# Keys in three tiles of 128 and a shared tile of 64, in place of four tiles of 112, in an attention-then-MLP kernel

## The chip, the cores and the metric

The kernel runs on one core of one Trainium2 chip. The metric is device microseconds of one execution, taken as the median of three runs. Smaller is better. The kernel reads its inputs from HBM in float32, works on them in bfloat16 on TensorE (PE) with float32 sums, and writes float32.

## What is computed

There are 8 batches of 12 heads; each head has 448 rows of 64 numbers. Queries and keys are normalised, attention follows, and the heads of a token, side by side (768 numbers), go through an MLP with a hard-swish.

```python
def rmsnorm(x, g):
    return x / np.sqrt(np.mean(x * x, axis=-1, keepdims=True) + 1e-06) * g
q_n, k_n = rmsnorm(q, g_q), rmsnorm(k, g_k)        # q, k, v: (8, 12, 448, 64)
scores = np.matmul(q_n, k_n.transpose(0, 1, 3, 2)) / np.sqrt(64)
attn = softmax(scores)                              # over the 448 keys
x = np.matmul(attn, v).transpose(0, 2, 1, 3).reshape(3584, 768)
h = x @ w_in                                        # w_in: (768, 2048)
out = (h * np.clip(h + 3.0, 0.0, 6.0) / 6.0) @ w_out  # w_out: (2048, 768)
```

## The kernel before

**Work by pairs and batches.** Two heads form a pair; there are 6 pairs to a batch and 48 in all, numbered `P`. Once the six pairs of a batch are through attention, its 448 token rows are complete and its part of the MLP can run. Attention of later batches and MLP of earlier ones are woven together on PE.

**One pair, step by step.** `load` brings queries, keys and values of the pair into SBUF, one transfer of 256 KB for each, on SP's queue. Partition `p` holds rows `4p` to `4p+3` of each head, so a head's 448 rows lie on 112 partitions by 4. `prep` squares (`sq`, L401 on ACT, L403 on POOL), sums (`ssq`, L410 on DVE), takes the power -1/2 by a logarithm and an exponential on ACT (`rs`, L415 and L418) and scales into bfloat16 (`qks`, L427, mostly POOL). It also casts the values into `va`, which has a 65th column of ones, so that the sum of the softmax falls out of the same product. `trans` turns queries and keys so that the 64 numbers of a head lie on partitions: for `P` under 13 with PE (L479) and a copy out of PSUM, later with a transposing DMA from SP (L455) and a scaling in place (L464 or L466). Head 0 lies on partitions 0 to 63 of `T`, head 1 on 64 to 127.

`score` takes one key tile (112 keys, loaded as 128 columns) of both heads: two matmuls of 64 rows, one on each half of the PE array, with 448 query columns each (L510). ACT takes the exponential of both at once, 112 partitions by 896 columns (`eT`, L519). `av` multiplies one key tile's exponentials by the values: for each of 2 heads and 4 query tiles one matmul of 65 columns that sums into `X` (L531). `finish` takes the reciprocal of the 65th column (`rd`, L547), scales (`xn`, L550) and transposes into `xT`, with PE and a copy for the first two batches (L566) and with a transposing DMA later (L557).

**The MLP.** `h_group` makes one of 16 blocks of 128 hidden columns for a batch: 6 matmuls of 448 columns (L587), a RELU on ACT (`ts`, L594), a product on DVE (`gT`, L597). `y_group` makes 128 output rows of two batches: two halves of 384 columns, 16 matmuls each (L618), a copy and a store (L639). `w_in` and `w_out` arrive in four chunks each. POOL issues them, in line with its arithmetic (L653, L658); the chunk of `w_out` with hidden blocks `4c` to `4c+3` is needed by the `c`-th four matmuls of every half.

**PSUM.** Two score tiles `S` of two banks each, the two-bank `X`, and two single banks `M` for the MLP. From pair 24 on, one score tile in four is put into `X` while that is free, so that up to three score tiles stand next to each other.

**Order.** Nothing is decided at run time. `Plan.add` records every operation with the engines that may do it and their planned costs; `WAY` says which of these engines takes it, and `ORDER` is the full list of operations as they are emitted. Each engine executes its own in that order, and a dependency keeps it so.

Of the kernel before, what the change touches and what calls it, by code (L numbers as in the profile page):

```python
# [21 lines left out]
WAY = {53: 1, 63: 2, 67: 1, 68: 1, 69: 1, 78: 1, 83: 1, 84: 1, 95: 1, 101: 1, 126: 1, 132: 2, 157: 1,  # L22
    163: 1, 183: 1, 188: 1, 225: 1, 231: 1, 233: 1, 245: 1, 250: 1, 256: 1, 276: 1, 358: 1, 365: 1, 377: 1,
    388: 1, 400: 1, 424: 2, 429: 1, 446: 1, 453: 1, 458: 1, 460: 1, 487: 1, 500: 1, 505: 1, 516: 1, 518: 1,
    533: 1, 625: 1, 636: 1, 676: 1, 683: 2, 709: 2, 714: 1, 728: 1, 729: 1, 755: 1, 761: 2, 766: 1, 793: 1,
    798: 1, 821: 1, 892: 1, 899: 2, 925: 2, 930: 1, 945: 1, 951: 2, 977: 2, 1003: 2, 1008: 1, 1023: 1,
    1029: 1, 1034: 1, 1061: 1, 1097: 1, 1134: 1, 1148: 1, 1182: 2, 1206: 1, 1212: 1, 1226: 1, 1251: 1,
    1257: 2, 1263: 1, 1398: 1, 1413: 1, 1420: 2, 1426: 1, 1440: 1, 1447: 1, 1453: 1, 1464: 1, 1465: 1,
    1491: 1, 1515: 1, 1516: 1, 1522: 1, 1549: 1, 1555: 1, 1579: 1, 1615: 1, 1620: 1, 1652: 1, 1673: 1,
    1693: 1, 1700: 1, 1706: 1, 1718: 1, 1724: 2, 1744: 1, 1751: 2, 1757: 1, 1781: 1, 1795: 1, 1832: 1,  # L30
    1893: 1, 1921: 1, 1932: 1, 1938: 1, 1958: 1, 1971: 1, 1979: 1, 1980: 1, 1986: 1, 1992: 1, 2057: 1,
    2062: 1, 2093: 1, 2098: 1, 2125: 1, 2145: 1, 2162: 1, 2169: 1}


class Plan:

# [8 lines left out]
    def add(self, ways, want, fn, reads=(), writes=(), load=(), since=0.0, soon=()):  # L49
        i = len(self.ops)  # L50
        self.way[i] = WAY.get(i, 0)
        eng, occ, fin = ways[self.way[i]]
        soon = dict(soon)
        preds = {}

        def after(p, lat):
            preds[p] = max(preds.get(p, 0.0), lat)

        for r in reads:
            if r in self.last:  # L60
                after(*self.last[r])
            self.readers.setdefault(r, []).append((i, fin))
        for w in writes:
            for p in self.readers.get(w, ()):
                if p[0] != i:
                    after(*p)
            if w in self.last:
                after(*self.last[w])
        for w in writes:
            self.last[w] = (i, soon.get(w, fin))  # L70
            self.readers[w] = []
        self.ops.append((eng, occ, fin, want, fn, preds, load, since))
        self.ways.append(ways)
        return i

    def emit(self, order):

        place = {i: n for n, i in enumerate(order)}
        assert len(place) == len(self.ops)
        for i, o in enumerate(self.ops):  # L80
            assert all(place[p] < place[i] for p in o[5])
        for i in order:
            self.ops[i][4](self.ops[i][0])
# [3 lines left out]
    8, 9, 20, 13, 21, 22, 15, 23, 11, 24, 28, 10, 25, 19, 29, 53, 26, 12, 30, 27, 14, 54, 31, 16, 55, 32, 33,  # L87
    34, 17, 58, 35, 56, 36, 83, 37, 92, 38, 78, 59, 39, 60, 40, 57, 62, 41, 18, 69, 42, 43, 44, 61, 45, 93,
    68, 66, 46, 73, 47, 67, 64, 123, 48, 101, 70, 49, 50, 74, 122, 65, 75, 71, 63, 77, 104, 72, 217, 102, 84,
    105, 76, 81, 85, 154, 51, 103, 112, 94, 124, 82, 79, 52, 86, 114, 80, 113, 153, 126, 115, 110, 87, 95,  # L90
    155, 135, 88, 111, 96, 91, 89, 136, 106, 116, 184, 117, 107, 133, 97, 118, 90, 143, 119, 185, 156, 108,
    134, 132, 120, 186, 144, 109, 141, 121, 248, 142, 145, 146, 166, 98, 1, 157, 164, 147, 167, 158, 148, 99,
    165, 174, 163, 149, 215, 137, 150, 159, 172, 100, 125, 387, 138, 151, 175, 127, 0, 139, 216, 173, 218,
    140, 187, 152, 195, 128, 197, 188, 129, 196, 176, 177, 178, 198, 130, 179, 189, 203, 160, 204, 205, 131,
    246, 180, 168, 181, 190, 206, 161, 169, 170, 247, 182, 171, 191, 183, 162, 228, 385, 226, 229, 207, 194,
    208, 386, 201, 227, 199, 192, 209, 416, 202, 210, 200, 236, 211, 234, 225, 212, 237, 230, 414, 219, 213,
    249, 259, 214, 231, 6, 220, 238, 260, 239, 193, 235, 445, 267, 2, 221, 232, 240, 222, 268, 241, 257, 223,
    242, 233, 243, 415, 258, 250, 261, 244, 262, 245, 265, 256, 251, 277, 266, 278, 224, 269, 279, 280, 281,
    443, 252, 396, 388, 253, 397, 263, 270, 271, 264, 255, 272, 398, 285, 286, 273, 287, 274, 288, 254, 289,
    401, 275, 444, 389, 402, 395, 399, 276, 390, 400, 3, 290, 282, 406, 291, 407, 5, 391, 403, 292, 392, 283,  # L100
    472, 405, 394, 297, 284, 298, 404, 393, 293, 299, 408, 294, 417, 502, 300, 425, 295, 418, 305, 426, 296,
    306, 4, 427, 419, 501, 301, 307, 302, 420, 430, 308, 428, 421, 303, 409, 422, 431, 313, 429, 424, 473,
    446, 314, 423, 304, 432, 410, 315, 411, 309, 433, 316, 310, 474, 434, 412, 321, 413, 311, 322, 312, 454,
    323, 531, 447, 435, 455, 436, 324, 317, 456, 448, 318, 329, 319, 503, 475, 459, 449, 457, 320, 450, 437,
    460, 438, 330, 452, 458, 439, 440, 453, 325, 331, 451, 461, 530, 332, 462, 441, 326, 476, 442, 463, 337,
    338, 477, 327, 7, 483, 339, 464, 328, 484, 621, 465, 504, 466, 340, 467, 478, 333, 485, 468, 482, 469,
    486, 345, 479, 487, 480, 488, 346, 489, 470, 622, 534, 490, 347, 471, 491, 334, 348, 481, 493, 492, 494,
    495, 335, 496, 512, 336, 647, 533, 497, 513, 341, 498, 342, 535, 514, 499, 515, 343, 517, 516, 344, 648,
    536, 505, 354, 537, 518, 506, 539, 349, 500, 350, 538, 507, 351, 508, 649, 509, 519, 520, 522, 523, 510,
    355, 521, 356, 511, 524, 541, 544, 625, 525, 542, 526, 527, 543, 357, 699, 540, 352, 358, 635, 624, 528,  # L110
    546, 353, 529, 547, 674, 366, 650, 626, 361, 548, 360, 651, 367, 627, 673, 676, 368, 652, 628, 532, 677,
    549, 632, 700, 633, 550, 630, 678, 551, 552, 369, 634, 629, 553, 362, 679, 554, 675, 370, 637, 653, 545,
    654, 661, 728, 363, 655, 638, 555, 378, 556, 656, 639, 379, 701, 636, 380, 687, 703, 680, 658, 752, 659,
    364, 681, 623, 640, 660, 726, 641, 365, 631, 642, 381, 702, 371, 729, 663, 382, 730, 751, 373, 664, 682,
    374, 665, 704, 375, 731, 889, 732, 684, 662, 705, 727, 685, 561, 643, 686, 562, 644, 645, 376, 706, 372,
    563, 734, 688, 689, 713, 377, 690, 666, 893, 667, 564, 668, 669, 725, 691, 557, 708, 683, 558, 646, 755,
    670, 671, 710, 657, 559, 890, 569, 733, 711, 560, 570, 672, 892, 707, 565, 712, 894, 891, 566, 571, 692,
    739, 693, 567, 694, 572, 695, 895, 915, 715, 896, 568, 716, 577, 696, 709, 578, 753, 717, 573, 383, 714,
    754, 574, 579, 736, 384, 697, 575, 737, 580, 718, 698, 719, 756, 720, 738, 585, 765, 586, 576, 757, 918,
    359, 721, 758, 741, 587, 722, 723, 742, 735, 581, 588, 759, 582, 724, 743, 740, 744, 593, 583, 941, 760,  # L120
    762, 584, 967, 763, 594, 944, 589, 903, 764, 897, 590, 968, 595, 745, 767, 591, 898, 916, 596, 768, 746,
    592, 747, 601, 919, 748, 769, 749, 602, 993, 766, 761, 597, 603, 920, 900, 750, 901, 770, 771, 772, 604,
    969, 773, 902, 598, 774, 775, 994, 970, 609, 921, 599, 899, 610, 922, 776, 924, 600, 905, 611, 908, 906,
    909, 612, 923, 605, 917, 904, 907, 606, 955, 617, 607, 618, 1019, 608, 945, 926, 619, 946, 942, 613, 927,
    910, 943, 911, 928, 620, 614, 996, 912, 929, 781, 947, 913, 948, 615, 997, 931, 925, 1020, 932, 934, 616,
    935, 950, 914, 782, 998, 933, 936, 949, 1021, 777, 783, 937, 999, 784, 778, 1000, 938, 952, 939, 779,
    1146, 1001, 789, 953, 956, 940, 790, 1002, 780, 954, 791, 951, 981, 1148, 971, 785, 1147, 786, 972, 957,
    787, 960, 958, 961, 1197, 788, 792, 1022, 930, 1196, 794, 793, 973, 1149, 959, 795, 1145, 796, 1023, 1150,
# [79 lines left out]
def kernel(  # L208
# [84 lines left out]
    for t in T_r:  # L293
        nc.vector.memset(t[:, S2:], 0.0)
    for t in eT_r:
        nc.vector.memset(t[:, :, S2:], 0.0)
# [485 lines left out]
```

## Time and profile before

| | |
|---|---|
| time of three runs | 429.72, 429.72, 430.66 us; median 429.72 us |
| span of the profiled execution, first to last instruction | 427.8 us |
| PE busy | 415.1 us (97%), granted clock 1.000 |
| ACT, DVE, POOL busy | 296.7, 219.6, 171.1 us |
| chain that ended last | PE 90%, ACT 4%, issue 2% |
| DMA | 67.77 MB, 158 GB/s over the span |

The profile records one execution, whose span is 427.8 us; no time of its own is listed beside that. The median of the three runs is 1.9 us above the span, and this is taken for what lies around the span (start and end of the program). PE's busy time is modelled from starts, since matmuls are pipelined: a matmul of 448 columns shows 353 ns by itself, while six of them in a row take 1.14 us in the chain, 190 ns each. Costs of PE are therefore read from the chain, not from the mean of a group.

### The profile page before, as it was taken

The numbers are of one execution on the slowest core, as the hardware profiler recorded it, in microseconds if no ns is written. First come the engines' busy times: TensorE is split into PE (matmuls) and PEld (weight loads), VectorE is DVE, ScalarE is ACT, GpSimd is POOL, SyncE is SP. The second block draws the span as 40 slices with busy tenths as digits, with TensorE's granted clock in tenths as the row PEclk, the third lists the DMA queues.
The fourth block names the chain that finished last, engine by engine and source line by source line (L and its number), as shares of the span: only waits on it lengthen the run. The fifth ranks groups of instructions, "written<-read, shape, count | busy, mean of one in ns | idle before, by whom it ended". The sixth has DMA issues, their size and how long they took to land.

```text
span 427.8 us, 9914 instructions
## 1 busy us (share of the span) xinstructions
PE 415.1 (97%) x3946; PEld 238.6 (56%) x3946; DVE 219.6 (51%) x405; ACT 296.7 (69%) x535; POOL 171.1 (40%) x188
## 2 busy tenths in 40 slices
PE   9678999999999999999999999999999999999996
PEld 8455455555555555555555555555555555655554
DVE  5665776547787965665545454434434332243211
ACT  5999898889998988968757977575575556222221
POOL 2899865874767866255524340312200000000000
PEclk9999999999999999999999999999999999999999
DMA  8999999698799999668565865352413221021113
GB/s 258 349 249 288 242 240 250 149 267 231 197 237 262 229 234 227 187 155 233 136 170 132 215 156 124 75 125 55 93 33 70 50 60 49 11 75 37 38 38 113
DMA packets 98931, 67.77 MB, mean 158 GB/s; under 512 B 53156, under 2 KB 95428, under 8 KB 98884
## 3 DMA queue, kind: packets, MB, share of 16 engines
q1 hardware_dynamic: 93248, 60.50, 54.5%
q0 software_dynamic: 5248, 6.29, 8.4%
q8 instruction: 31, 0.51, 0.5%
q10 hardware_dynamic: 388, 0.34, 0.3%
q14 instruction: 16, 0.13, 0.1%
HBM read 50.23 MB, written 11.01 MB: 143 GB/s over the span
## 4 chain that ended last, share of the span: by engine, by line
PE 90%; ACT 4%; issue 2%; DVE 1%; DMA 1%; POOL 1%; SPq 0%; POOLq 0%
PE M L587 32%; PE M L618 29%; PE X L531 10%; PE S L510 8%; PE S L618 5%; ACT eT L519 2%; PE X L587 1%; DMA qk<-in_k_dram 1%; PE S L587 1%; PE X L510 1%; PE X L618 1%; POOL qks L427 1%; DVE gT L597 0%; SPq L388 0%; ACT ts L594 0%
## 5 line engine op out<-in xcount | busy, mean ns | idle before, releaser
L519 ACT ACTIVATE eT<-S 112x896 bf16<-112x896 f32 x168 | 148.1, 918 | 13.8 <-PE S L510 13.3
L587 PE MATMUL M<-xT,w_in_sb 128*128 128x448 bf16 x714 | 153.2, 353 | 0.8 <-ACT xT L347 0.4
L618 PE MATMUL M<-w_out_sb,gT 128*128 128x384 bf16 x752 | 135.9, 326 | 0.0
L597 DVE SCALAR_TENSOR_TENSOR gT<-ts,M 128x448 bf16<-128x448 f32 x119 | 73.4, 619 | 101.9 <-ACT ts L594 101.7
L427 POOL TENSOR_TENSOR qks<-qk,rs 112x512 bf16<-112x512 f32 x94 | 96.2, 1043 | 65.5 <-DMA T<-qks 31.9
L618 PEld LDWEIGHTS <-gT 128*128 128x128 bf16 x912 | 84.8, 98 | 61.9 <-issue 9.7
L594 ACT ACTIVATE ts<-M 128x448 f32<-128x448 f32 x119 | 64.8, 548 | 61.0 <-PE M L587 59.8
L587 PEld LDWEIGHTS <-w_in_sb 128*128 128x128 bf16 x768 | 69.9, 98 | 65.7 <-issue 10.9
L403 POOL TENSOR_TENSOR sq<-qk 112x512 f32<-112x512 f32 x56 | 57.7, 1041 | 43.4 <-DMA qk<-in_k_dram 18.2
L531 PEld LDWEIGHTS <-eT 112*128 112x128 bf16 x1536 | 57.1, 97 | 18.1 <-issue 8.2
L410 DVE TENSOR_REDUCE ssq<-sq 112x16 f32<-112x1024 f32 (+1 forms) x50 | 57.9, 1172 | 15.8 <-ACT sq L401 11.9
L531 PE MATMUL X<-va,eT 112*128 112x65 bf16 x1536 | 62.3, 194 | 1.0 <-DVE xT L349 0.8
L510 PE MATMUL S<-T 64*128 64x448 bf16 x336 | 47.3, 354 | 2.1 <-ACT eT L519 1.5
L550 DVE TENSOR_TENSOR xn<-X,rd 112x512 bf16<-112x512 f32 x48 | 33.2, 691 | 1.6
L351 POOL CAST va<-vf 112x512 bf16<-112x512 f32 x20 | 12.3, 613 | 41.1 <-PE X L531 38.8
L510 PEld LDWEIGHTS <-T 64*128 64x128 bf16 x384 | 12.8, 94 | 27.9 <-issue 21.0
L401 ACT ACTIVATE sq<-qk 112x512 f32<-112x512 f32 x40 | 24.9, 629 | 4.7 <-DMA qk<-in_q_dram 2.3
L347 ACT COPY y<-M 128x384 f32<-128x384 f32 x26 | 12.5, 481 | 18.4 <-PE M L618 18.1
L547 DVE RECIPROCAL rd<-X 112x8 f32<-112x8 f32 x48 | 9.8, 204 | 28.1 <-PE X L531 27.9
L349 DVE COPY y<-M 128x384 f32<-128x384 f32 x21 | 11.7, 555 | 22.8 <-PE M L618 22.6
L519 ACT ACTIVATE eT<-X 112x896 bf16<-112x896 f32 x24 | 22.1, 923 | 0.0
L618 PE MATMUL S<-w_out_sb,gT 128*128 128x384 bf16 (+1 forms) x128 | 21.8, 316 | 0.0
(58 smaller groups left out, 188.3 us busy)
## 6 DMA issues: line engine op xcount, KB each, us to landing
qk<-in_q_dram SPq DMA_DIRECT2D x47, 256.0 KB, 4.2
qk<-in_k_dram SPq DMA_DIRECT2D x47, 256.0 KB, 4.0
vf<-in_v_dram SPq DMA_DIRECT2D x47, 256.0 KB, 4.8
w_in_sb<-in_moe_w_in_dram POOLq DMA_DIRECT2D x4, 768.0 KB, 12.7
w_out_sb<-in_moe_w_out_dram POOLq DMA_DIRECT2D x4, 768.0 KB, 14.5
out_dram<-y SPq DMA_DIRECT2D x7, 336.0 KB, 2.8
out_dram<-y SPq DMA_DIRECT2D x8, 288.0 KB, 2.7
out_dram<-y SPq DMA_DIRECT2D x8, 240.0 KB, 3.4
```

Of the source, the lines that this page charges most:

```text
L401: em(nc.scalar.square(out=sq[:, i], in_=x))
L403: em(nc.gpsimd.tensor_tensor(out=sq[:, i], in0=x, in1=x, op=A_MULT))
L410: em(nc.vector.tensor_reduce(out=ssq[:, s].rearrange("p i n -> p (i n)"), in_=sq[:, s].rearrange("p i (n d) -> p (i n) d", d=D), axis=AX_X ...
L427: em((nc.vector if e == DVE else nc.gpsimd).tensor_tensor(out=qks[:, i].rearrange("p t h d -> p h t d"), in0=qk[:, i].rearrange("p h (t d) ...
L510: em(nc.tensor.matmul(out=ps[:, a, 0:S], lhsT=qkT[r, S + t * TP:S + t * TP + 128], rhs=qkT[r, 0:S], start=True, stop=True))
L519: em(nc.scalar.activation(out=eT[:, t, 0:S2].rearrange("p (a s) -> p a s", a=2), in_=ps[0:TP, :, 0:S], func=EXP, bias=0.0, scale=1.0))
L531: em(nc.tensor.matmul(out=X_ps[:, a, i * E1:(i + 1) * E1], lhsT=eT[:, t, c:c + 128], rhs=va[:, a, t, :], start=(t == 0 and i == 0), stop=( ...
L550: em(nc.vector.tensor_tensor(out=xn[:].rearrange("p i a d -> p a i d"), in0=xv[:, :, :, 0:D], in1=rd[:].unsqueeze(3).to_broadcast([TP, 2, ...
L587: em(nc.tensor.matmul(out=ps[:, 0:S], lhsT=w_in_sb[:, kt, f * 128:(f + 1) * 128], rhs=xT[:, kt, :], start=(kt == 0), stop=(kt == NKT - 1)))
L594: em(nc.scalar.activation(out=ts[:], in_=ps[:, 0:S], func=RELU, bias=0.5, scale=1.0 / 6.0))
L597: em(nc.vector.scalar_tensor_tensor(out=gT[:, f, e * S:(e + 1) * S], in0=ts[:], scalar=1.0, in1=ps[:, 0:S], op0=A_MIN, op1=A_MULT))
L618: em(nc.tensor.matmul(out=ps[:, 0:nc0], lhsT=gT[:, f, i * 128:(i + 1) * 128], rhs=w_out_sb[:, f, c0:c0 + nc0], start=(f == 0), stop=(f == ...
```

## The change

Keys are no longer laid out as 4 tiles of 112. Keys and values are loaded by two transfers each: partitions 0 to 63 get rows `7p` to `7p+3`, partitions 64 to 127 get rows `7p+3` to `7p+6`, so one row in seven is there twice. Of the four tiles of 128 that result, head 0 uses tiles 0, 1, 2 and the upper half of tile 3, head 1 uses tiles 1, 2, 3 and the lower half of tile 0: three tiles of 128 keys and 64 left over, 448 in all. The two sets of 64 left over are copied into a block-diagonal tile `kd` of 128 by 128 (two small copies a pair, on POOL or DVE), so that one matmul over all 128 rows scores both heads' rest (`rest`), and one exponential of 448 columns follows. Their `av` has matmuls of 64 rows, with the two heads on the two halves of the array in turn. Queries are cut into tiles of 128 columns of the 448 (the last one is half padding), tiles that were 112 partitions are 128, and the transposes move blocks of 128. Queries are scaled in place of keys. Score tiles are no longer put into `X`; each score tile is an operation of its own. `ORDER` and `WAY` are new throughout.

```diff
-    def score(slots, want):
-        parts = [(P, t, *((X_ps, ("X",)) if wide else sbank())) for P, t, wide in slots]
+    def score(P, m, want):
+        ps, res = sbank()
...
+                c = (m + a) * 128
+                em(nc.tensor.matmul(
+                    out=ps[:, a, 0:S], lhsT=qkT[r, 1, c:c + 128], rhs=queries(P)[r],
+                    start=True, stop=True))
...
+    def rest(P, want):
...
+            em(nc.tensor.matmul(
+                out=ps[:, 0, 0:S], lhsT=kd[:], rhs=queries(P), start=True, stop=True))
...
+            em(nc.scalar.activation(out=eR[:, 0:S], in_=ps[:, 0, 0:S], func=EXP, bias=0.0, scale=1.0))
...
     def av(P, m, want):
...
+            for i in range(T):
                 for a in range(2):
+                    if m == NM:
+                        r = slice(0, PU) if a else slice(PU, 128)
+                        lhsT, rhs = eR[r, i * 128:i * 128 + 128], va[r, a, 0 if a else T - 1, :]
+                    else:
+                        c = a * S + i * 128
+                        lhsT, rhs = eT[:, m, c:c + 128], va[:, a, m + a, :]
...
+        def f_kd(e):
+            for a in range(2):
+                r = slice(a * 64, a * 64 + 64)
+                c = 0 if a else 512 - PU
+                o = 0 if a else PU
+                copy(e, kd[r, o:o + PU], dst[r, 1, c:c + PU])
...
+            for u, r, step in [(0, slice(0, PU), SU), (1, slice(PU, 128), SU)] if i else [(0, slice(0, whole), T)]:
...
+    def pair_scores(P, w, step):
+        for n, (d, m) in enumerate([(0, 0), (0, 1), (0, NM), (0, 2), (1, 0), (1, NM), (1, 1), (1, 2)]):
+            if P + d < NP:
+                (rest(P + d, w + n * step) if m == NM else score(P + d, m, w + n * step))
```

Here `T` is 4, `S` is 448, `PU` is 64, `SU` is 7 and `NM` is 3 (also the index of the rest).

## The prediction

> **What bounds the kernel now.** I read the busy table and the slices first, then the chain that ended last, piece by piece, and last the stretches in which PE is not the chain.
>
> ```profile
> PE 415.1 (97%) x3946; PEld 238.6 (56%) x3946; DVE 219.6 (51%) x405; ACT 296.7 (69%) x535; POOL 171.1 (40%) x188
> PE   9678999999999999999999999999999999999996
> ACT  5999898889998988968757977575575556222221
> PE 90%; ACT 4%; issue 2%; DVE 1%; DMA 1%; POOL 1%; SPq 0%; POOLq 0%
> ```
>
> After the first slices PE is full and is the chain; ACT is near full only early. So PE work counts one to one later, and the other engines count in the first 43 us. A piece of the chain (start, duration, what) gives PE's prices:
>
> ```profile
> 212.56 2.27 PE M L587 x12
> 214.84 0.48 PE S L510 x4
> 215.32 0.19 PE X L510 x2
> 215.51 1.24 PE M L587 x6
> 216.75 1.30 PE M L618 x8
> 218.05 0.49 PE X L531 x16
> ```
>
> A matmul of 448 columns costs 189 ns (2.27/12), one of 384 costs 162.5. A pair of half-array score matmuls costs the same 0.19 us (the x2): the two overlap fully. The first four cost 0.48 where 0.38 is due, and the six behind them 1.24 where 1.14 is due: a block of half-array matmuls costs 0.2 us for going in and out. An `av` matmul costs 30.2 ns. With these prices, the instruction list after the last `xT` transpose of batch 0 (it ends at 42.93 us) sums to 380.8 us; PE's last matmul ends at 424.38, which is 381.4. The price list holds.
>
> The start is different:
>
> ```profile
> 20.00:40.00 20.00, 16.06 (x271) 10.49 (x267) 12.63 (x22) 18.80 (x36) 19.34 (x22) 1.00 1.15 277
> 80.00:100.00 20.00, 20.00 (x208) 10.91 (x204) 12.89 (x24) 17.38 (x34) 16.96 (x18) 1.00 1.10 262
> 42.72 0.21 PE X L566 x4
> ```
>
> (columns: PE, PEld, DVE, ACT, POOL busy, clock, DMA share, GB/s). From 20 to 40 us ACT and POOL are full and PE is not. And one more stream runs under it: the weights.
>
> ```profile
> 23.18 0.88 POOL L653 DMA_DIRECT2D w_in_sb<-in_moe_w_in_dram  x1
> ...
> 61.90 0.80 POOL L658 DMA_DIRECT2D w_out_sb<-in_moe_w_out_dram  x1
> q0 software_dynamic: 195, 0.29, 78.5%
> q0 software_dynamic: 7, 0.01, 1.8%
> 72.64 2.11 PE M L618 x12
> ```
>
> The q0 lines are 60 to 62 us and 72 to 74 us. In windows of 2 us q0 carries 0.25 to 0.29 MB while the loads compete, about 5.85 us for a chunk of 0.786 MB, with hardly a gap from 36 us until it ends at about 72. The first `y_group` needs the last `w_out` chunk at its 13th matmul, at about 74.0. The slack is 2 us or less.
>
> **PE's work, part by part.** Counted from that 13th matmul to the end, before has 1216 `av` matmuls, 300 score matmuls and 63 half-array blocks; after has 888 full and 296 half-array `av`, 216 score, 36 `rest` matmuls and 60 blocks; `h` and `y` are equal, after has 8 PE transposes more.
> - Scores: 300 x 94.6 ns = 28.4 us become 216 x 94.6 + 36 x 189 = 27.2. A `rest` costs what a pair of score matmuls cost. Saves 1.2, since slightly more is already done.
> - Blocks: 3 x 0.2 = 0.6 saved. The new half-array `av` mostly stand beside scores in the order, so they open few blocks of their own. Transposes: 8 x 50 ns = 0.4 lost.
> - `av`: 1216 x 30.2 = 36.7 us become 888 x 30.2 = 26.8, and 296 half-array ones. No row shows these. If they overlap as score pairs do, 15.1 ns each, 4.5 us; if not at all, 30.2 ns, 8.9 us. The nearest row is the score pair (same halves, full overlap), but with 448 columns, not 65, so I take 20 ns, 5.9 us. Saves 4.0 (1.0 to 5.4). It could even lose, if weights for half the array load slower; the weight loads of 64 rows take 94 ns against 97 for 112, which speaks against that.
>
> Sum: 5.4 us, 2.4 to 6.8. I use 5.3.
>
> The Trainium skill (TensorE: Matmul & The Clock Gate, "Wait — 56ns, not 53.3ns?") says that start-to-start never falls below about 25 ns, however few columns; no row here goes below 30. If that floor also held for alternating halves, the 296 would cost 7.4 us and the sum would be 3.9 in place of 5.3, an estimate.
>
> **The start.** ACT: from the first exponential to the last one of pair 5, before has 24 of 0.815 us, five squares, twelve small `rs` steps and five copies or casts, 26.5 us of work in 27.5 us of time (11.53 to 39.05). After has 18 of 0.815 and 6 of about 0.43 (a 448-column RELU steps at 0.44), five squares, eleven `rs` steps, no copies: 21.8 us. DVE takes over: up to the sixth `xT` copy its list is six small and several full `ssq` (1.21 each), scalings and copies (0.4), `kd` (two of about 0.12), `rd` and `xn` (0.85 a pair): 30.7 us of work after about 4.7 us, so 35.4 at the earliest. Its waits before 20 us were 4.0 us; I add 3.6. The last `xT` transpose falls at about 38.6 rather than 42.9: 4.3 earlier (2 to 6).
>
> Much of that is given back. Between it and the 13th `y` matmul the new order has 31.3 us of PE work, so PE could be there at 69.9. POOL's new list puts 7 squares, 14 scalings, 3 casts, 4 `kd` copies, a `w_in` and a `w_out` issue, 25 us, before the second `w_in` issue, which before was at 23.18; since the first scaling can't start before about 10, it is at 34 to 36. The first `w_out` goes out at about 28.4 and flows from 31. From there seven chunks follow without a gap: 31.3 + 7 x 5.85 = 72.3. So the 13th matmul can run at about 73.3, against 74.0 before: the start brings 0.7 us, not 4.1. The second `w_in` chunk, needed at 44.1, lands at 43.5 by the same sum; POOL two us later would stop PE there, but that would overlap the later wait.
>
> **Loads, queues, other engines.** SP issues 96 more transfers: at 0.37 to 0.47 us each, some 40 us over 300 us, on a queue that is about 70% taken between 150 and 200 us. Loads are planned 30 us ahead, and behind them stand transposes planned 35 us ahead; that lead hides it. Without it, one late transfer costs its 2 to 6 us landing once. The Trainium skill (DMA: Bandwidth & Descriptors, "Rules for kernel authors") advises against splitting a transfer into partition halves, as both use the same engines; by that rule the loads gain nothing and the sum stays. POOL and DVE share 96 `kd` copies, 12 us in all, beside work; a late one would stop PE at `rest`, since PE's order is fixed. ACT does 48 x (0.815 - 0.43) = 18 us less; off the chain after 43 us it brings nothing itself. Transposes of 128 in place of 112 rows I put at nothing: the transposing issue already takes 1.2 us and lands in 2.8 to 3.5.
>
> **New waits.** Before, with `X` as third score tile, PE had at least 2.1 us of other work between two uses of a score tile. By the same prices from 60 us on the shortest is now 1.0 us, and 27 of 142 are under 2.0. A full exponential alone takes 0.82 plus the way to it, and a RELU may stand ahead. I put 1.0 us for this (0 to 8).
>
> **Sum.** 0.7 + 5.3 - 1.0 = 5.0 us. Span 427.8 - 5.0 = 422.8; with the 1.9 around it 424.7 us, against the median of 429.72.
>
> **Rivals.**
> - *The weights don't hold the start back* (POOL runs ahead, or the queue is faster): the full 4.1 us stays, 421.3; with full overlap of the halves 419.8. For: q0 alone reached 0.33 MB in 2 us. Against: loads compete in nearly every window. Chance 0.13.
> - *The half-array `av` don't overlap*: 2.4 in place of 5.3, 427.6. That part of the change then does not do what it says. Chance 0.20; half of that ends within 0.3%.
> - *Slower: score tiles come free late.* PE stands at a score because its tile still waits for the exponential, and everything behind it on PE waits too. It decides from 0.27 us for each of the 27 short gaps (7.3 us in all); at 0.35 us the time is 433. For: ACT is at 0.87 from 80 to 100 us with 0.44 us RELUs in between, and one row before already shows ACT releasing a score. Against: ACT has 18 us less to do. Chance 0.23.
> - *Forecast as worked out*, 422 to 428: 0.44.
>
> **How the numbers follow.** What can be told from no change is 0.3%, 1.3 us. Faster: 0.44 + 0.13 + 0.10 = 0.67. Same: 0.10. Slower: 0.23. The range goes from 419.5 (first rival with full overlap) to 432.5, which takes in most of the third; about 0.18 stays outside.
>
> **What would show it.** Right: the chain with eight half-array `av` in 0.12 to 0.2 us; the last `xT` transpose of batch 0 near 38.6; q0 busy without a gap to 72 and PE idle before the 13th `y` matmul; after that at most 1 us of PE idle on ACT. Wrong: that transpose after 42; `PE S <- ACT eT` of several us; an 8-fold `av` at 0.24.

## The result, and the profile after

The changed kernel takes 479.36 us (median of 476.69, 477.84, 480.87 and 482.48), against 429.78 us for the kernel before beside it: a ratio of 1.114 (95% interval 1.108 to 1.120). The forecast was 424.7 us with a range up to 432.5, so it missed by 55 us, and on the wrong side.

The profiled execution took 476.69 us, its span is 474.9 us. These are the lines of its page that answer to the first ones shown of before (busy times, PE and ACT in 40 slices, the chain), with the granted clock:

```profile
PE 425.0 (89%) x3880; PEld 243.1 (51%) x3880; DVE 239.8 (50%) x464; ACT 280.5 (59%) x532; POOL 178.7 (38%) x237
PE   6679789986978989897999969998999999999995
ACT  5768568765976657674775746565567554232201
PEclk9979899998999999999999989999999999999999
PE 50%; DMA 18%; SPq 10%; POOL 6%; issue 6%; DVE 6%; ACT 3%; ACTq 0%; POOLq 0%; DVEq 0%
```

In before PE was full from the fourth slice on. Now it has gaps until about 340 us. The chain shows what fills most of them: DMA 18% and SP's queue 10%, where before had 1% and 0%; POOL and DVE, with 6% each, had 1%. So most of the loss is not on an engine that computes. PE stands idle for 474.9 - 425.0 = 49.9 us (before: 12.7), and in several slices its clock is granted at less than 1.

The stretches shown of before, again (PE, PEld, DVE, ACT, POOL busy, clock, DMA share, GB/s):

```profile
20.00:40.00 20.00, 14.50 (x224) 10.13 (x222) 13.17 (x30) 12.82 (x23) 11.98 (x15) 0.83 0.91 207
80.00:100.00 20.00, 18.51 (x189) 10.45 (x186) 8.95 (x18) 15.26 (x31) 11.90 (x17) 1.00 0.69 144
```

From 20 to 40 us ACT was busy for 18.80 and POOL for 19.34 us before; now nothing is full, and the transfers bring 207 GB/s in place of 277. The loads, line by line (shortest / median / longest issue in ns, first and last start), before and then after:

```profile
L388 SPq DMA_DIRECT2D qk<-in_q_dram x48: 367/424/1602, 0.7 to 257.1; - x48
L388 SPq DMA_DIRECT2D qk<-in_k_dram x48: 367/420/776, 1.3 to 256.5; - x48
```

```profile
L395 SPq DMA_DIRECT2D qk<-in_k_dram x96: 595/605/1487, 1.3 to 342.5; - x96
L395 SPq DMA_DIRECT2D vf<-in_v_dram x96: 595/605/1027, 9.7 to 376.3; - x96
L395 SPq DMA_DIRECT2D qk<-in_q_dram x48: 368/582/1637, 0.7 to 341.1; - x48
```

Half a load takes SP's queue longer to issue (0.605 us) than a whole one did (0.420). The timeline of SP in after shows what that does at the start (start, duration, several in a row as one line):

```profile
0.74 0.46 SPq L395 DMA_DIRECT2D qk<-in_q_dram  x1
1.26 2.06 SPq L395 DMA_DIRECT2D qk<-in_k_dram  x3
...
4.00 1.90 SPq L395 DMA_DIRECT2D qk<-in_k_dram  x3
5.94 1.11 SPq L395 DMA_DIRECT2D qk<-in_q_dram  x2
7.10 2.56 SPq L395 DMA_DIRECT2D qk<-in_k_dram  x4
9.70 1.25 SPq L395 DMA_DIRECT2D vf<-in_v_dram  x2
```

The queue has no gap. 128 KB every 0.65 us is about 200 GB/s, and 204 GB/s is what the first 20 us carry (before: 301). Added up from SP's timeline, issues take about 77% of the first 50 us and 93% of the stretch from 100 to 150 us; in before it was 41% and 81%. The engines behind wait for loads (who waited for this line, us and times):

```profile
  POOL sq L411: 45.3, 18
  ACT sq L409: 24.4, 16
  POOL va L357: 15.7, 4
```

In before these waits were 29.4 (POOL `sq`), 4.4 (ACT `sq`) and 2.3 us (`va`).

### The profile page after: what moved, and what is told of

Read it like the earlier page. It is cut to its first block, busy times and chain, and to the rows that moved or that the text cites. A ratio compares the mean times of both kernels' runs of the same rounds, so it can differ in the third digit from the quotient of the medians.

```text
span 474.9 us, 9952 instructions
## 1 busy us (share of the span) xinstructions
PE 425.0 (89%) x3880; PEld 243.1 (51%) x3880; DVE 239.8 (50%) x464; ACT 280.5 (59%) x532; POOL 178.7 (38%) x237
## 4 chain that ended last, share of the span: by engine, by line
PE 50%; DMA 18%; SPq 10%; POOL 6%; issue 6%; DVE 6%; ACT 3%; ACTq 0%; POOLq 0%; DVEq 0%
PE M L627 19%; PE M L658 15%; DMA qk<-in_k_dram 8%; SPq L395 7%; DMA qk<-in_q_dram 5%; PE X L570 5%; PE S L658 4%; POOL qks L435 3%; PE S L533 3%; DMA T<-qks 3%; POOL sq L411 2%; DMA vf<-in_v_dram 2%; DVE ssq L418 2%; DVE gT L637 1%; SPq L463 1%
## 5 line engine op out<-in xcount | busy, mean ns | idle before, releaser
L538 ACT ACTIVATE eT<-S 128x896 bf16<-128x896 f32 x144 | 128.3, 914 | 28.9 <-PE S L533 27.6
L435 POOL TENSOR_TENSOR qks<-qk,rs 128x512 bf16<-128x512 f32 x94 | 97.3, 1048 | 62.7 <-ACT rs L426 40.0
L411 POOL TENSOR_TENSOR sq<-qk 128x512 f32<-128x512 f32 x51 | 52.9, 1040 | 81.0 <-DMA qk<-in_k_dram 32.7
L418 DVE TENSOR_REDUCE ssq<-sq 128x16 f32<-128x1024 f32 (+1 forms) x50 | 58.3, 1170 | 31.2 <-POOL sq L411 16.9
L570 PEld LDWEIGHTS <-eT 128*128 128x128 bf16 x1152 | 50.3, 100 | 17.9 <-issue 5.1
L570 PE MATMUL X<-va,eT 128*128 128x65 bf16 x1152 | 56.4, 198 | 0.0
L409 ACT ACTIVATE sq<-qk 128x512 f32<-128x512 f32 x45 | 28.2, 627 | 30.8 <-DMA qk<-in_q_dram 16.2
L589 DVE TENSOR_TENSOR xn<-X,rd 128x512 bf16<-128x512 f32 x48 | 33.1, 690 | 5.8 <-DMA xT<-xn 4.6
L554 ACT ACTIVATE eR<-S 128x448 bf16<-128x448 f32 x48 | 25.8, 542 | 13.8 <-PE S L550 13.5
L570 PE MATMUL X<-va,eR 64*128 64x65 bf16 x384 | 14.3, 194 | 16.4 <-POOL va L357 4.7
```

The lines of the kernel that those rows point to most:

```text
L411: em(nc.gpsimd.tensor_tensor(out=sq[:, i], in0=x, in1=x, op=A_MULT))
L418: em(nc.vector.tensor_reduce(out=ssq[:, s].rearrange("p i n -> p (i n)"), in_=sq[:, s].rearrange("p i (n d) -> p (i n) d", d=D), axis=AX_X ...
L435: em((nc.vector if e == DVE else nc.gpsimd).tensor_tensor(out=qks[:, i].rearrange("p t h d -> p h t d"), in0=qk[:, i].rearrange("p h (t d) ...
L538: em(nc.scalar.activation(out=eT[:, m, 0:S2].rearrange("p (a s) -> p a s", a=2), in_=ps[:, :, 0:S], func=EXP, bias=0.0, scale=1.0))
L570: em(nc.tensor.matmul(out=X_ps[:, a, i * E1:(i + 1) * E1], lhsT=lhsT, rhs=rhs, start=(m == NM and i == 0), stop=(m == NM - 1), skip_group_ ...
L589: em(nc.vector.tensor_tensor(out=xn[:].rearrange("p i a d -> p a i d"), in0=xv[:, :, :, 0:D], in1=rd[:].unsqueeze(3).to_broadcast([128, 2, ...
```

## The experiments

**Theory 1:** the loss is the loading by halves, since SP's queue takes 0.6 us for each of four halves (1a), or since a transfer of 64 partitions moves slowly (1b). **Theory 2:** it is the new order itself, with later weights and other places for SP's transfers. A third suspect came up on the way: DVE's `kd` copies. Times are medians; before took 430.9 to 431.7 us beside them.

**e1: whole loads in after.** At the place of the two halves stands one transfer of 128 partitions; at the place of the second half, nothing.

```diff
-            for u, r, step in [(0, slice(0, PU), SU), (1, slice(PU, 128), SU)] if i else [(0, slice(0, whole), T)]:
+            for u in (0, 1) if i else (0,):
...
+                    if u == 0:
+                        em(nc.sync.dma_start(out=dst[0:whole], in_=...))   # rows 4p to 4p+3
```

> The kernel after, in its own order, but K and V of a pair each come in one transfer of 128 partitions from contiguous rows, as before (so keys and values of the upper half are not those that the reference asks for; all work after the load is as in after). Theory 1, the two half transfers are the loss (0.605 us of SP's queue for each, and 8 in flight carry half the bytes): 422 to 432 us, a whole load issues in 0.37 to 0.45 us, the shares of SPq and of DMA in the chain fall from 10% and 18% to 1% each. Theory 2, the new order itself is late (weights issued at 50 to 63 us, transposes placed late): 465 us or more, with the same idle stretches of PE between 40 and 280 us.

Measured: 447.4 us (ratio to before 1.038, 1.035 to 1.041). 32 us come back by this alone, with the order unchanged. In the chain SPq falls to 2%, but DMA only to 10%. Theory 1 has most of the loss, but 16 us above before remain, which neither theory had said.

**e2: halves from contiguous rows.** As after, but the second half starts 256 rows on and the row step is 4.

> The kernel after, with K and V still in two transfers of 64 partitions, but from contiguous rows (the second half starts after 256 rows; again not the keys that the reference asks for). If the row step of 7 makes an issue dear, the halves issue in 0.2 to 0.4 us and the time falls to 425 to 440 us. If a transfer of 64 partitions is dear by itself, they stay at 0.6 us and the time at 470 to 480 us. If the order is the loss (theory 2), 465 us or more whatever the issue takes.

Measured: 480.5 us, issue 0.6 us. The step of 7 rows costs nothing that shows. The time alone would suit theory 2 too; that it is the 64 partitions that make an issue dear, e9 shows.

**e3: the same two transfers, one per head.** Each brings 2 runs of 64 rows to 128 partitions.

```diff
+                        em(nc.sync.dma_start(out=dst[:, u], in_=bass.AP(
+                            h.tensor, h.offset, [[(SU - T) * D, 2], [SU * D, PU], [1, T * D]])))
```

> The kernel after, with the same number of transfers and bytes (two of 128 KB for each K and V), cut the other way: each brings one head to all 128 partitions, its source in two runs of 64 rows a step of 7 apart. It computes the reference. If the number of transfers is the loss, 465 to 480 us and issues of 0.6 us. If the form of 64 partitions is the loss, issues of 0.3 to 0.45 us and 425 to 445 us. If the step of 7 rows is the loss, no change: 0.6 us and 470 to 480 us.

Measured: 801.6 us, far outside all three expectations. The issue alone is 0.50 us at its shortest, so another cost had to be there; e9 measures it.

**e4: the halves in before.** Before's own order, K and V in two transfers of 64 partitions, step 7.

```diff
+                for u in (0, 1):
+                    em(nc.sync.dma_start(out=dst[64 * u:64 * u + 64], in_=bass.AP(
+                        rows.tensor, rows.offset + 3 * u * D, [[7 * D, 64]] + [list(d) for d in rows.ap[1:]])))
```

> The kernel before, in its own order, with each K and V load cut into two transfers of 64 partitions with the row step of 7, as in after (the keys and values are then not those that the reference asks for). Theory 1: the loss of after appears in before, 460 to 480 us, with SPq and DMA at 15% or more of the chain. Theory 2 (order): 430 to 440 us, since the loads of before are planned far ahead.

Measured: 463.7 us (1.076, 1.073 to 1.079): 33 us lost in an order that was not touched, with DMA at 11% and SPq at 8% of the chain. As theory 1 had it.

**e5 and e6: DVE's `kd` copies.** In e1 two of these copies of 64 by 64 numbers stand on DVE for 4.68 us together, while POOL works (DVE, then POOL, in the timeline of e1):

```profile
54.19 0.61 DVE L635 SCALAR_TENSOR_TENSOR gT<-ts,M 128x448 bf16<-128x448 f32 x1
54.72 4.68 DVE L355 COPY kd<-T 64x64 bf16<-64x64 bf16 x2
59.43 0.39 DVE L355 COPY xT<-X 128x448 bf16<-128x448 bf16 x1
```

```profile
55.20 1.03 POOL L409 TENSOR_TENSOR sq<-qk 128x512 f32<-128x512 f32 x1
56.19 0.60 POOL L357 CAST va<-vf 128x512 bf16<-128x512 f32 x1
56.74 0.82 POOL L696 DMA_DIRECT2D w_out_sb<-in_moe_w_out_dram  x1
57.58 1.05 POOL L433 TENSOR_TENSOR qks<-qk,rs 128x512 bf16<-128x512 f32 x1
58.57 0.80 POOL L696 DMA_DIRECT2D w_out_sb<-in_moe_w_out_dram  x1
59.39 1.05 POOL L409 TENSOR_TENSOR sq<-qk 128x512 f32<-128x512 f32 x1
```

In the chain they take 1.48 and 3.11 us; the first ends at 56.28, with POOL's `sq`, the second at 59.40, with POOL's weight issue. Their median in e1 is 0.18 us. The kernel already had a slower form of copy on DVE for `va`, which also sums (`accum_out`). e5 is e1, and e6 is after, with that form for `kd`:

```diff
+                if e == DVE:
+                    em(nc.vector.tensor_scalar(
+                        kd[r, o:o + PU], dst[r, 1, c:c + PU], 1.0, None, A_MULT, A_ADD, accum_out=junk_t[r]))
```

> The kernel of e1 (whole loads; keys and values of the upper half are not the reference's), with the 42 kd copies that DVE makes in the accumulating form that the kernel already uses for va. Theory: DVE's plain copies from SBUF to SBUF wait for POOL (two of them took 4.6 us at 55 us in e1, 0.18 us is their median) and this late DVE is part of the 17 us that e1 is above before: then no kd copy takes over 0.3 us and the time falls from 447 to between 435 and 443 us. Rival: the late weights (third w_in chunk issued at 52.7 us, before at 43.0) and the order are all of it: 445 to 449 us.

> The kernel after, complete, with nothing changed but the form of DVE's 42 kd copies. They take 17.3 us in after against 7.5 us at their median, so at most 10 us lie there. If the loads are late first (theory 1), most of that is beside other waits: 472 to 479 us.

Measured: e5 440.7 us, 6.7 below e1; no `kd` copy takes longer than 0.218 us. e6 478.9 us, no different from after (479.4). So the copies are a real cost with whole loads. In after none shows: e6's two runs lie 5.9 us apart, so a few us could hide there. The Trainium skill (SBUF — State Buffer, "SBUF: two separate sides") says that GpSimd (POOL) shares a pair of ports with those DVE operations that run in a two-port mode or read two inputs from SBUF, under an exclusive lock, held for a whole instruction. The end of the first copy agrees with it. The second stands beside four POOL instructions in a row, which a lock given back after each does not explain by itself. Why the form that also sums does not wait was not shown.

**e7 and e8: the upper halves from ACT's or POOL's queue.**

```diff
-                    em(nc.sync.dma_start(out=dst, in_=rows))
+                    em((nc.scalar if u and P > 3 else nc.sync).dma_start(out=dst, in_=rows))   # e8: nc.gpsimd
```

> The kernel after, complete, with e6's copies and from the fifth pair on the upper halves (partitions 64 to 127) of K and V issued from ACT's queue in place of SP's. Theory 1a, the time that SP's queue takes to issue (0.605 us a half, 3.0 us a pair): SP's share goes to 1.8 us a pair, and the time to 440 to 455 us, the rest of the way to e5 being lost to 0.6 us issues on ACT. Theory 1b, the half transfers themselves are slow on the DMA engines or in flight: 465 us or more.

> As e7, with the upper halves issued from POOL's queue. POOL's issue of a weight chunk takes 0.8 to 0.9 us; 88 of them add some 50 to 75 us to POOL's 179 us. Theory 1a: 440 to 460 us. Theory 1b: 465 us or more. POOL may become late for the scaling of qks, which would show as POOL in the chain.

Measured: e7 468.7 us, e8 477.0 us, where e6 has 478.9. Both lie in the range that 1b was given and above that of 1a. But an issue takes 0.60 us on ACT and 0.62 on POOL too, and stands there in front of the work that these engines do in order: POOL's busy time rises from 178 to 230 us, and the chain of e8 has POOL's `qks` at 8.0% (e6: 4.0%). Since the same 0.6 us only moves to another engine, I don't take these two as a verdict for 1b: the halves land 3.7 to 4.4 us after their issue here, the whole loads of before 4.0 to 4.8 us. Why e7 gains no more was not settled.

**e9: what each form of load costs by itself.** Before, with loads of K after its end, four of each form, each waiting for the one ahead. "Spacing" is (last start - first start) / 3, that is one issue and one landing.

> The kernel before, complete, and after its last store 16 forms of a load of K from SP's queue, four times each into the same tile, so that each waits for the one ahead (the total time is longer by these and tells nothing). It measures what the issue and the landing of each form cost by themselves. If the number of partitions decides the issue, 64 partitions take 0.60 us with 1, 2 or 4 heads and with short rows alike, and 96, 112 and 128 take 0.34 to 0.42. If the bytes or pieces decide, 64 by 4 heads (256 KB) takes twice the time of 64 by 2. The form of e3 (2 by 64 rows to 128 partitions), which took 0.5 us to issue there, lands far later than the 4 us of a whole load: e3's 801 us would come from that.

| partitions x heads (rows of 1 KB) | KB | issue, median us | spacing us |
|---|---|---|---|
| 128 x 2 | 256 | 0.378 | 2.63 |
| 112 x 2 | 224 | 0.328 | 2.60 |
| 96 x 2 | 192 | 0.312 | 2.40 |
| 64 x 2, lower or upper half, step 4 or 7 | 128 | 0.596 to 0.608 | 2.60 to 2.67 |
| 64 x 4 | 256 | 0.598 | 3.47 |
| 64 x 1 | 64 | 0.476 | 2.10 |
| 32 x 2 | 64 | 0.315 | 1.93 |
| 128 x 4 | 512 | 0.379 | 3.57 |
| e3's form: 2 by 64 rows to 128 partitions | 128 | 0.520 | 5.10 |
| the same rows in 64 by 2 order | 128 | 0.540 | 2.43 |

As expected, 64 partitions are dear with two heads and with four: 0.6 us, and also 0.596 us with two heads and short rows (512 B). Not as expected, one head takes less, 0.476 us, though still more than one head on 128 partitions (0.337). Two lines of this run, 128 by 2 and 64 by 2:

```profile
L760 SPq DMA_DIRECT2D qk<-in_k_dram x4: 367/378/415, 427.4 to 435.3; - x4
L766 SPq DMA_DIRECT2D qk<-in_k_dram x4: 595/608/717, 458.0 to 465.9; - x4
```

Half the bytes take as long from start to start as all of them. And e3 is settled: its form takes 5.1 us for 128 KB, the same rows walked in another order 2.43. The Trainium skill (DMA: Bandwidth & Descriptors, "Why a DMA increments its semaphore by 16 and not by 1") says that the slowest dimension of the pattern decides on how many engines a transfer runs; 2 there would mean two engines, 64 sixteen. The trace agrees: while e3's form runs, the 16 DMA engines are busy for one to two tenths on average and never move more than about 50 GB/s; in the other order it is up to eight tenths and about 300 GB/s.

**e10: whole loads, but SP kept busy.** e5, with a transfer of 64 partitions by 128 B ahead of each of the three loads.

> The kernel of e5 (whole loads, kd copies in the accumulating form; not the reference's keys), with one small transfer of 64 partitions by 2 by 64 B ahead of each of the three loads of a pair: 9 KB of data a pair, but 0.6 us of SP's queue each if 64 partitions decide. SP then spends 3 us a pair on loads as in after, while the loads themselves are whole. Theory 1a (SP's issue time is the loss): 465 to 480 us. Theory 1b (half transfers move slowly): 440 to 450 us.

Measured: 515.0 us, more than after itself, with whole loads. With whole loads, then, more transfers and more time on SP's queue are enough to make a loss. But it overshoots: the whole loads behind the small ones take 0.59 us to issue, which makes 3.9 us of SP a pair and not 3, and the small transfers also made SP wait 47.5 us for their own landing. So the run shows the direction and not the size.

**e11: whole loads for the first 12 pairs only.**

> The kernel of e6 (after, kd copies in the accumulating form), with whole contiguous loads of K and V for pairs 0 to 11 only (for these pairs not the reference's keys), halves from pair 12 on. It splits the 38 us between e6 (478.9) and e5 (440.7) into the first 100 us, where no transposing transfer is on the queue, and the rest. PE's idle time in after and e1 says about half and half: 457 to 463 us. If the start alone sets it (a lost lead is never made up), 440 to 447 us.

Measured: 468.6 us: 10 of the 38 us between e6 and e5 come from the first 12 pairs, 28 from the rest. More lies in the later part than expected (457 to 463 us).

**e12: two pairs in one transfer.** K and V as 64 partitions by 4 heads, six buffers for them; it computes the reference.

> The kernel after, complete, with e6's copies, and from the third pair on K and V of two pairs brought together by two transfers of 64 partitions by 4 heads (256 KB each), with six buffers for K and V in place of five; it computes the reference. Transfers per pair fall from 5 to 3. If an issue of 64 partitions takes 0.6 us whatever it carries, SP spends 1.65 us a pair and the time is 438 to 450 us (theory 1a). If half transfers move slowly (1b), 460 us or more.

Measured: 462.4 us, the fastest form of the changed kernel that was run and computes the reference, and slower than before by 7% (1.047 to 1.098). SP spends about 2.0 us a pair here (two issues of 0.61, `q` at 0.58, three gaps of 0.05), but 22 us above e5 is more than SP's time explains, and 462.4 us is what 1b was given. Such a transfer also takes 3.5 us alone against 2.6, lands 5.1 us (K) after its issue against 4.0 in before, and needs the buffers of two pairs free. Which of these it is was not settled.

**e13 to e16: number of transfers against time on SP's queue.** The control e13 is before, with each transposing transfer replaced by two plain copies of 64 partitions. Then K and V are cut in three ways:

```diff
+                for r in (slice(0, 64), slice(64, np)):                    # e14
+                for r in (slice(0, 96), slice(96, np)):                    # e15
+                for r in [slice(x, x + 32) for x in range(0, 128, 32)]:    # e16
+                    em(nc.sync.dma_start(out=dst[r], in_=rows[r]))
```

> A control: the kernel before with each of its 71 transposing transfers replaced by two plain copies of 64 partitions of the same tiles (T and xT then hold untransposed data, so the output is not the reference's; every instruction behind them is as in before). By e9 two such issues take 1.2 us of SP's queue, like the 1.22 us of a transposing one. If it stands for before, 426 to 434 us.

> The control of e13 with K and V cut into two loads of 64 partitions, contiguous: 2.8 us of SP's queue a pair in place of 1.26. As e4 did in before: 20 to 35 us above the control.

> The control of e13 with K and V cut into two loads of 96 and 32 partitions: as many transfers as e14, but 0.31 us each, 1.7 us of SP's queue a pair. If the number of transfers is the loss, 20 to 35 us above the control like e14; if SP's issue time is, 0 to 6 us above it.

> The control of e13 with K and V cut into four loads of 32 partitions each: 9 loads a pair, 0.315 us each, 2.9 us of SP's queue a pair, as much as e14. If SP's issue time is the loss, it comes out within 8 us of e14. If the form of 64 partitions is slow in another way than by its issue, it lies far below e14; if the number of transfers is the loss, far above it.

SP's time per pair is the sum of the median issues, and 0.05 us between two.

| run | loads a pair | issue of one K part, us | SP's time a pair, us | time, us | above the control |
|---|---|---|---|---|---|
| e13 whole | 3 | 0.420 | 1.45 | 431.35 | 0 |
| e15 96 + 32 | 5 | 0.441 | 2.43 | 439.76 | 8.4 |
| e14 64 + 64 | 5 | 0.606 | 3.25 | 465.68 | 34.3 |
| e16 4 x 32 | 9 | 0.425 | 4.26 | 506.97 | 75.6 |

The issues of e14, e15 and e16:

```profile
L392 SPq DMA_DIRECT2D qk<-in_k_dram x94: 595/606/1830, 1.2 to 283.6; - x94
```

```profile
L392 SPq DMA_DIRECT2D qk<-in_k_dram x94: 311/441/1799, 1.2 to 260.9; - x94
```

```profile
L392 SPq DMA_DIRECT2D qk<-in_k_dram x188: 311/425/1900, 1.2 to 327.8; - x188
```

The control stands for before (1.0006, 0.998 to 1.004). e14 loses what e4 lost. e15 has the same number of transfers and bytes as e14 and loses a quarter of it. e15 and e16 fell outside their expectations, because on a busy queue 32 partitions, and 96, take 0.425 to 0.44 us and not e9's 0.31; by their own issues they follow one curve with e14. Over 48 pairs the added time on SP is 47, 86 and 135 us, and the loss 8, 34 and 76: some 35 to 40 us are hidden, and beyond that 0.66 to 0.85 us are lost for each microsecond added.

Theory 1b can be checked in the same runs, by the time from issue to landing (the last number, in us; e13, e14, e16):

```profile
qk<-in_k_dram SPq DMA_DIRECT2D x47, 256.0 KB, 4.3
qk<-in_k_dram SPq DMA_DIRECT2D x94, 128.0 KB, 3.1
qk<-in_k_dram SPq DMA_DIRECT2D x188, 64.0 KB, 2.4
```

The more a run loses, the sooner its transfers land. In e14 even a second half, issued 0.65 us behind the first, is there 3.75 us after the first one's issue, before a whole load would be. Slow transfers are thus not the loss, and 1a accounts for it in before: SP's queue is the resource, and its time decides, not the number of transfers by itself. In after, e1 and e5 show that the halves are the loss, but remove both suspects at once. For 1a speak SP's 3.25 us a pair, as in e14, with a like loss (32 us against e1, 38 between e6 and e5), and the landing of the halves, 3.6 us (K) and 3.2 us (V) after their issue, where the whole loads of before took 4.0 and 4.8. e7, e8 and e12 took time off SP's queue and gained less than 1a said; that stays open.

**e17 and e18: what whole loads still leave.** e17 is e5 with plain copies for the transposing transfers. e18 gives Q and K six buffers in place of five.

```diff
-    NQK, NV, NSQ, NRS, NQS, NVA, NT, NE, NXN, NXT, NTS, NY = 5, 5, 2, 4, 3, 4, 4, 2, 2, 2, 2, 3
+    NQK, NV, NSQ, NRS, NQS, NVA, NT, NE, NXN, NXT, NTS, NY = 6, 5, 2, 4, 3, 4, 4, 2, 2, 2, 2, 3
```

> A second control: the kernel of e5 (after's order, whole loads, kd copies in the accumulating form) with its transposing transfers replaced by two plain copies of 64 partitions each, as in e13 (neither the keys nor the transposed tiles are the reference's). If it stands for e5, 437 to 444 us.

> The control of e17 with six buffers for Q and K in place of five, the order kept but for operations that the deeper ring needs ahead of others. If what whole loads still leave above before (10 us) is SP standing at a load whose buffer is not free, with transfers queued behind, the time is 5 to 8 us below e17. If it is the order of the work itself (weights, DVE's list), within 2 us of e17.

Measured: 438.4 us and 431.3 us. SP's waits for a buffer, e17 and then e18 (us in total, times, longest):

```profile
SPq L393 <- POOL qks L433: 63.7, 21, 8.1
```

```profile
SPq L399 <- POOL qks L439: 20.3, 9, 7.0
```

This fits: SP had stood at loads whose buffer was not free, with the transfers behind them held up. (e18 also moves a few operations ahead, which was not tried by itself.) The 7.1 us are all that e17 lay above before (e18: 0.9986, 0.996 to 1.002). In this order, then, the queue needs room to run ahead as well as few entries; what a sixth buffer alone does for loads by halves was not tried. e18 also shows the most that this order gave in these runs, without transposing transfers and with whole loads: no gain over before.

## Why the prediction was wrong, step by step

**Where the 47 us are.** e18 executes the same 3880 matmuls at a granted clock of 1.000, and its PE is busy for 413.9 us. Against before's span of 427.8: PE's work -1.2 (413.9 - 415.1), a lower clock +11.1 (425.0 - 413.9; 413.9 / 0.976, the mean clock granted in after, is 424.1), idle PE +37.2 (49.9 - 12.7). That is 47.1, and the span is 474.9.

**The step that failed: loads.** The prediction put 96 more transfers "at 0.37 to 0.47 us each, some 40 us over 300 us, on a queue that is about 70% taken", and went on: "that lead hides it". The price was taken from whole loads, though the thing priced was another form. It is 0.605, and it replaces the old price too: (3.25 - 1.45) x 48 = 86 us, twice what was put. And the cover was asserted from the planner's lead times, not read from the queue; the 70% are those of 150 to 200 us, while from 100 to 150 us the queue was taken for about 81%. 40 us would nearly have fitted: e15 added 47 us to SP in before and lost 8.4. With 86 us it doesn't. The bound that went with it, "2 to 6 us landing once" for a late transfer, failed as well: the loss recurs, 17.3 us of it by the 13th `y` matmul and 29.8 us behind it. The page that was cited there, with its advice against splitting a transfer into partition halves, was read as "gains nothing, the sum stays". e4 shows 33 us lost by it.

**The start.** With loads in time it comes out near the forecast, but not by the path that was worked out. Start of the 13th `y` matmul, after and then e18:

```profile
91.33 1.46 PE L658 MATMUL M<-w_out_sb,gT 128*128 128x384 bf16 x8
```

```profile
72.65 1.46 PE L666 MATMUL M<-w_out_sb,gT 128*128 128x384 bf16 x8
```

The forecast was 73.3 us, against 74.0 in before. In e18 it is 72.65, and the last `xT` transpose of batch 0 ends at 40.3 (forecast 38.6). In after it is 91.33, and that transpose starts only at 52.03. The prediction had PE ready at 69.9 and held until 73.3 by weights that flow without a gap. In e18 PE is busy all the time from that transpose to the 13th matmul, 32.4 us where 31.3 were counted. The stretch from 40 to 60 us (columns as above):

```profile
40.00:60.00 20.00, 20.00 (x201) 10.90 (x199) 15.13 (x34) 17.43 (x33) 17.46 (x20) 1.00 1.18 242
```

The weights do have a gap: q0 carries only 0.05 and 0.06 MB in the two windows of 2 us from 64 to 68 us, since POOL issues the last chunk at 65.42, and its last packets come just before 72 us. So the weights were there when PE came, and PE's own work set the 72.65. That it lies so near to 73.3 is luck: a later transpose and more work made up for a wait that did not come. So 17.3 us of the loss had arisen by the 13th `y` matmul, and 29.8 us come later.

**PE's work.** It was oversized by 2 us. From the 13th `y` matmul to the end PE is busy for 350.4 us in before and 347.1 in e18: 3.3 us saved, in the bounds of 2.4 to 6.8 that were given, not the 5.3 that were used. e18 does not keep it: from there to the end PE is idle for 10.8 us, in before for 3.4, and that takes up what the start and the work had gained. The new operation was priced well (after, in its full stretch):

```profile
388.92 0.19 PE S L550
392.84 0.48 PE S L533 x4
393.33 0.12 PE X L570 x8
395.26 0.24 PE X L570 x8
```

A `rest` costs 0.19 us. Eight half-array `av` beside scores cost 0.12, that is 15 ns each. The halves do overlap: the rival against it falls, and so do the 25 ns each that the prediction weighed as a floor. (0.24 is eight full ones.) At 15 ns the prediction's own sum would be 6.8, so its other terms are 3.5 us too large together; which of them was not looked into.

**Score tiles.** They were put at 1.0 us, with a rival up to 8, and PE's waits for them are 2.4 us in all in after (1.4 on `eR`, 1.0 on `eT`) and 0.7 in e18, where loads are in time; before had 1.5. The slower rival had the right sign and the wrong mechanism. That a load could be the late thing was in the text only as one transfer, once.

**`kd` copies.** They were put at 12 us "beside work". Hidden they are in after (e6), but not with loads in time: 6.7 us in e5 against e1. The prediction had 0.12 us for one on DVE and did not ask what POOL does at that moment.

## What to carry to other kernels

Price a transfer by its own form, and price the queue that issues it as an engine: add up its issues per unit of work before and after, and compare with the time that the unit has. A cover that comes from a plan ("issued 30 us ahead") is worth only as much as the queue's own slack; read that slack in the queue's timeline. When a transfer has to be cut, measure the cuts first: here 96 + 32 partitions cost a quarter of what 64 + 64 cost.

## What the runs showed of the hardware that was not expected

- The issue time on SP's queue does not follow the bytes, nor grow steadily with the partitions: 0.31 us for 32 or 96 partitions, 0.38 for 128, and 0.60 for 64, by two or four heads (e9; one head on 64 took 0.476). On a busy queue 32 and 96 took 0.425 to 0.44 (e15, e16). Why 64 is dear was not found.
- A transfer whose outermost dimension is 2 took 5.1 us where the same bytes in another order took 2.43 (e9), and cost 320 us over the kernel (e3 against after).
- A DVE copy of 64 by 64 numbers, 0.18 us at its median, took up to 3.1 us beside POOL's instructions (e1); the form that also sums never took over 0.22 (e5).
- On the whole PE was granted a lower clock in runs in which it idled more, so that an idle PE cost more than its idle time: with 16.6 us idle the mean was 1.000 (e18), with 49.9 us 0.976 (after), with 309.7 us 0.789 (e3), where the same matmuls kept PE busy for 491 us in place of 414. The busy share of one stretch does not tell it: in after the clock was 0.83 with 14.50 us busy of 20 (20 to 40 us), but 1.00 with 13.25 (the first 20 us). What sets it was not looked into.
